# Second MLP of a fused attention + two-MLP kernel: one written order to the end, products gathered into one run per pair, middle block in reverse, six buffers on the way out

## The chip, the cores and the metric

The kernel runs on one core of a Trainium2 chip. The metric is the device time of one execution in microseconds (us). Engines: PE (TensorE, matrix products; its weight loads are listed as PEld), DVE (VectorE), ACT (ScalarE), POOL (GpSimd) and SP, whose queue issues the DMAs here (rows of it are named SPq).

## What is computed

Attention with a sliding window, then two MLPs one after the other, over 2304 tokens of 512 features and 2048 hidden units:

```
attn = softmax(scale*q.k^T + bias, window 128) . v     -> x, 2304 x 512
h = x @ w_in1;    x1 = (s * relu(h)^2 + b) @ w_out1
h = x1 @ w_in2;   out = relu(h)^2 @ w_out2
```

The change concerns the last line alone.

## The kernel before

**Number format.** A value is kept as two float32r halves, high and low, and each product of two values is three matmuls (high.high, high.low, low.high). Weights arrive as 64-bit words and are converted on ACT, DVE and POOL once.

**Tiles.** The second MLP takes the 2304 tokens in three blocks n = 0, 1, 2 of 768 (two halves of 384), and the 2048 hidden units in eight pairs of units of 128, y = 0 to 7. So there are 24 steps k = 8n + y. A step has
- seven first-layer products p1, p2, p6, p5, p7, p4, p3 (a seven-product scheme in place of eight), each of 6 matmuls of 384 columns. p1, p6, p7 and p4 add up in one PSUM bank (`px`), p2, then p5 and p3 in another (`py`). There is one bank of each, so the next step's p1 overwrites what the last one's p4 left in `px`;
- between them the readers of these banks: ACT copies m, u, v out of `px` (tiles `tm`, `tu`, `r_all`) and DVE adds them to `py`; ACT applies relu (j0 to j3, tiles `tr`);
- q0 to q3: DVE squares `tr`, ACT and DVE write its two halves;
- twelve second-layer groups F0 to F11, each of 3 matmuls of 512 columns, which add into six PSUM banks `po` over all eight steps of a block. F0 to F2 need q0, F3 to F5 q1, F6 to F8 q2, F9 to F11 q3. F of step k-1 runs beside the products of step k.

**Waits between products and readers.** p6 adds into the bank that m copies, so it waits for m; p7 waits for u, p4 for v in the same way; p5 overwrites what j0's DVE add reads, p3 adds to what j1's reads; the next step's p1 waits for j2's relu and its p2 for j3's DVE add.

**Weights.** Six pieces per pair, 2.75 MB as float32r halves, are made in block 0 (letters l load, a and b convert, S sums, c split) and stored to DRAM (d). Three sets of places in SBUF hold the pieces of three steps; set k mod 3 serves step k. In blocks 1 and 2 every pair is loaded again (w): 16 pairs.

**Inputs.** Y loads a block's input, Z scales it on ACT, T forms differences on DVE, V splits into halves (ACT copy, DVE subtract of 768 columns); V4 and V3 write the operands of p4 and p3.

**Ways out.** After the eighth step of a block, O0 to O5 copy the six `po` banks to SBUF (ACT and DVE in turn, tiles `ob`) and SP writes them to `out`. O0, O2 and O4 take tag `raw` with 2 buffers, O1, O3 and O5 tag `st` with 3.

**What sets the order.** PE always keeps the order of the program text. The other queues keep it only where a flag (`pinned`) is set; elsewhere a scheduler places their instructions. Block 0 is written out by hand in the table `HANDOVER`, with the flag set: it runs while the first MLP ends, up to some 666 us. Steps 8 to 23 come from the loop at L927, with the flag cleared (L915), and the scheduler may also lift work of the loop into the table's stretch. All instructions are recorded under one line, L29, a helper; so rows are told apart by tiles. In names, `wd` is the DRAM copy of weights, `m2...` the places in SBUF (weights, input halves and the halves of units alike), `acc` the first MLP's result in DRAM.

Of the kernel before, what the change touches and what calls it, by code (L numbers as in the profile page):

```python
# [8 lines left out]
F32 = mybir.dt.float32  # L9
# [6 lines left out]
P = 128  # L16


class InOrder:
# [63 lines left out]
    V1.2 p7.5 W80 V1.6 b7.3 F6.0 d4.5 c7.4 p7.7 d5.3 v7 j7.1 q6.2 w8.0 q7.0 c7.5 w8.5 w9.2 T1.4 w9.1 V1.5 d7.5 V1.7 F6.1 F6.2
    w8.3 F6.3 F6.4 p7.4 p7.3 d7.1 w10.2 w8.4 V1.4 F6.5 V1.3 d6.4 j7.2 F6.6 w10.3 F6.7 F6.8 j7.3 q7.1 F6.9 F6.10 F6.11 w9.4
    q7.2 d6.5 w9.5 d7.4 w10.1 q7.3 w10.0
# [6 lines left out]
def attention_mlp2_kernel(ctx, tc, first0, first1, qkv0, qkv1, qkvt, w_in1, w_out1, s_in, b_in, w_in2, w_out2, out):  # L92
# [604 lines left out]

    BIG, HT, NP = 3 * BLK, 3 * P, NF // 2
# [72 lines left out]
    def load_weights(k, i):  # L771
        sync.dma_start(place_of_weight(k, i).bitcast(F32), wd[k % NP][i])

    def load_input(n, q):
        c, t = divmod(q, 2)
        y = yf[(n, q)] = bp.tile([P, 2, HT], F32, tag="yf", name=f"yf{n}{q}", bufs=5)
        c = slice(2 * c, 2 * c + 2)
        if t == 0:
            sync.dma_start(y[:, :, :BLK], acc_dram[3 * n][:, c, :])
            sync.dma_start(y[:, :, BLK:], acc_dram[3 * n + 1][:, c, :P])  # L780
        else:
            sync.dma_start(y[:, :, :P], acc_dram[3 * n + 1][:, c, P:])
            sync.dma_start(y[:, :, P:], acc_dram[3 * n + 2][:, c, :])
# [211 lines left out]
```

## Time and profile before

| | |
|---|---|
| runs | 934.68 us median of three (934.24 to 935.93) |
| profiled execution | 935.84 us, its span 934.0 us |
| PE busy | 904.3 us, 97% |
| DVE, ACT, POOL busy | 548.4 us, 502.8 us, 102.0 us |
| granted PE clock | 0.99 over the span |

The page lists busy time by engine and forty slices of the span; in all of the second MLP's slices but the last PE shows 9 (90% or more). So the readings that matter are PE's own rows in order of time (start, length of a merged row, and in brackets the idle time before it with what ended it), and beside them the queues that PE waited for. Matmuls overlap in the rows: the distance between two starts is the time that a group costs, not its listed length.

### The profile page before, as it was taken

What the parts mean: (1) busy time and instruction counts of PE and PEld (TensorE: products, weight loads), DVE (VectorE), ACT (ScalarE), POOL (GpSimd) and SP (SyncE); (2) the same over time, 40 slices, a digit from 0 to 9 for tenths busy, and PEclk for the clock granted to TensorE, in tenths of its full rate; (3) what the DMA queues carried; (4) which work ended last, traced back from release to release, by engine and by line L of the source; (5) the groups of instructions that cost most, each with busy time, mean ns of one, the idle gap of its engine ahead of it and who ended that gap; (6) DMA issues with size and microseconds to landing.
All of it is one profiled execution on the core that took longest, in us unless ns stands there. A gap on an engine that the chain in (4) does not pass through costs nothing.

```text
span 934.0 us, 14553 instructions
## 1 busy us (share of the span) xinstructions
PE 904.3 (97%) x5304; PEld 779.1 (83%) x5304; DVE 548.4 (59%) x1321; ACT 502.8 (54%) x1123; POOL 102.0 (11%) x164
## 2 busy tenths in 40 slices
PE   5899999999999999999999999999999999999997
PEld 3789998877787788788898998887889898989896
DVE  6998776455456445544376987787853436443432
ACT  6978775444344444544366876775653335333332
POOL 4343220000000000000022313222000000000000
PEclk8899999999999999999999999999999999999999
DMA  8533523111012101220226665859996656766312
GB/s 315 194 127 133 180 69 114 46 47 40 18 35 91 46 24 46 63 81 16 68 68 217 233 208 184 316 182 349 335 411 203 186 186 183 236 200 192 101 46 68
DMA packets 70216, 136.75 MB, mean 146 GB/s; under 512 B 8576, under 2 KB 36480, under 8 KB 70144
## 3 DMA queue, kind: packets, MB, share of 16 engines
q1 hardware_dynamic: 70144, 135.82, 43.8%
q8 instruction: 42, 0.69, 0.3%
q14 instruction: 30, 0.25, 0.1%
HBM read 103.29 MB, written 32.51 MB: 145 GB/s over the span
## 4 chain that ended last, share of the span: by engine, by line
PE 72%; DVE 11%; ACT 8%; DMA 5%; issue 3%; POOL 0%; SPq 0%; ACTq 0%; DVEq 0%; POOLq 0%
PE ha L29 17%; PE oa L29 17%; PE po L29 16%; PE px L29 8%; PE py L29 6%; PE s L29 6%; DMA st<-w_in 3%; DVE st L29 3%; ACT st L29 2%; DMA st<-w_out 2%; PE u L29 2%; DVE tr L29 1%; PE s_t L29 1%; DVE m2wih L29 1%; DVE r_all L29 1%
## 5 line engine op out<-in xcount | busy, mean ns | idle before, releaser
L29 POOL TENSOR_TENSOR st<-st 128x256 int32<-128x256 int32 x128 | 93.9, 759 | 273.1 <-DVE st L29 247.3
L29 DVE SCALAR_TENSOR_TENSOR r_all<-ha,r_all 128x256 f32<-128x256 f32 (+1 forms) x96 | 52.7, 553 | 103.2 <-ACT r_all L29 103.1
L29 ACT ACTIVATE r_all<-ha 128x256 f32<-128x256 f32 (+1 forms) x96 | 46.3, 485 | 102.4 <-PE ha L29 97.9
L29 ACT ACTIVATE st<-st 128x512 int32<-128x512 uint32 (+3 forms) x100 | 79.7, 813 | 11.0 <-DMA st<-w_in 5.9
L29 PE MATMUL oa<-ga,woh 128*128 128x256 f32 x384 | 72.5, 288 | 0.1
L29 DVE TENSOR_TENSOR tr<-tr 128x384 f32<-128x384 f32 x96 | 55.0, 574 | 22.6 <-ACT tr L29 22.6
L29 ACT ACTIVATE pr<-pr,nd 128x256 f32<-128x256 f32 (+1 forms) x102 | 48.0, 475 | 29.7 <-DVE nd L29 27.6
L29 PEld LDWEIGHTS oa<-ga,woh 128*128 128x128 f32 x384 | 60.1, 191 | 4.6 <-issue 3.5
L29 ACT ACTIVATE tr<-tr 128x384 f32<-128x384 f32 x72 | 37.7, 524 | 40.4 <-DVE tr L29 40.2
L29 PE MATMUL oa<-ga,wol 128*128 128x256 f32 x192 | 54.3, 283 | 0.0
L29 DVE SCALAR_TENSOR_TENSOR st<-st 128x512 int32<-128x512 int32 (+1 forms) x50 | 41.6, 840 | 11.4 <-ACT st L29 10.8
L29 DVE TENSOR_TENSOR tr<-py,tm 128x384 f32<-128x384 f32 x24 | 13.3, 555 | 44.6 <-PE py L29 43.0
L29 DVE TENSOR_TENSOR m2woh<-tr,m2woh 128x384 fp32r<-128x384 f32 x48 | 27.4, 571 | 20.1 <-ACT m2woh L29 18.3
L29 PE MATMUL po<-m2wih,m2woh 128*128 128x512 f32 x144 | 36.6, 395 | 1.3 <-ACT ob L29 0.9
L29 PE MATMUL po<-m2wih,m2wil 128*128 128x512 f32 x144 | 37.8, 392 | 0.0
L29 ACT ACTIVATE m2woh<-tr 128x384 fp32r<-128x384 f32 x48 | 25.2, 525 | 23.2 <-DVE tr L29 22.7
L29 PE MATMUL po<-m2wih,m2wol 128*128 128x512 f32 x144 | 37.6, 392 | 0.0
L29 PE MATMUL ha<-x0h,wih 128*128 128x256 f32 x128 | 37.3, 292 | 0.0
L29 PE MATMUL ha<-x0h,wil 128*128 128x256 f32 x128 | 36.4, 284 | 0.6 <-DVE wil L29 0.6
L29 PEld LDWEIGHTS oa<-ga,wol 128*128 128x128 f32 x192 | 36.7, 191 | 0.0
L29 PE MATMUL ha<-x0l,wih 128*128 128x256 f32 x128 | 36.2, 283 | 0.0
L29 PE MATMUL po<-m2wil,m2woh 128*128 128x512 f32 x144 | 36.0, 393 | 0.0
(606 smaller groups left out, 2404.6 us busy)
## 6 DMA issues: line engine op xcount, KB each, us to landing
m2wih<-wd SPq DMA_DIRECT2D x32, 512.0 KB, 4.6
m2woh<-wd SPq DMA_DIRECT2D x22, 512.0 KB, 4.5
st<-w_out SPq DMA_DIRECT2D x20, 512.0 KB, 4.4
st<-w_in SPq DMA_DIRECT2D x8, 1024.0 KB, 6.4
st<-w_in SPq DMA_DIRECT2D x16, 512.0 KB, 4.4
wd<-m2wih SPq DMA_DIRECT2D x16, 512.0 KB, 6.9
m2wil<-wd SPq DMA_DIRECT2D x16, 512.0 KB, 4.6
st<-w_out SPq DMA_DIRECT2D x6, 1024.0 KB, 7.5
```

Source lines behind the costliest of these rows:

```text
L29: ins = op(*args, **kw)
```

## The change

1. `HANDOVER` loses all stores d5, d6 and d7 and all loads w8, w9 and w10, as well as V1.4, V1.3, q7.1, q7.2 and q7.3; these V and q now stand in the loop's first turn. Nothing else in the table changes its place. Two of its lines, before and after:

```
    d5.1 j6.0 T1.3 T1.2 d6.0 b6.3 F4.6 q5.3 a7.1 d6.1 F4.7 F4.8 F4.9 a7.0 c6.5 b7.1 F4.10 F4.11 p6.5 d5.0 p6.7 F5.0 l7.2 d6.2
    j6.0 T1.3 T1.2 b6.3 F4.6 q5.3 a7.1 F4.7 F4.8 F4.9 a7.0 c6.5 b7.1 F4.10 F4.11 p6.5 p6.7 F5.0 l7.2 b7.0 F5.1 F5.2 v6 p6.4 d4.4
```

2. The flag stays set to the end, so ACT, DVE and SP keep the written order in the loop too.
3. The loop runs to k = 24. One turn is: p4 and p3 of step k-1, then p1, p2, p6, p5, p7 of step k in one run, then all twelve F of step k-1 in one run. q2 is done inside the products, q3, q0 and q1 behind them.
4. In block 1 the pairs go 7, 6, ..., 0. Pairs 7, 6, 5 are still in place from block 0, and pairs 0, 1, 2 are in place when block 2 begins, so five pairs are loaded per block and not eight. Stores d7, d6, d5 are issued in turns 8, 9, 10.
5. O0 to O5 get six buffers (`raw`, `st` and one of `yf`); the last bank's two column halves get a tile each.
6. In block 2 the short tail block of tokens (its rows go out in two DMAs per copy) comes first and not last.

```diff
+    def pair_of(k):
+        n, y = divmod(k, NP)
+        return NP - 1 - y if n == 1 else y
@@ place_of_weight, load_weights
-        tag, n = UNITS[k % 3][2 * i:2 * i + 2]
+        tag, n = UNITS[pair_of(k) % 3][2 * i:2 * i + 2]
-        sync.dma_start(place_of_weight(k, i).bitcast(F32), wd[k % NP][i])
+        sync.dma_start(place_of_weight(k, i).bitcast(F32), wd[pair_of(k)][i])
+    def blocks_of(n):
+        return (LAST, 3 * n, 3 * n + 1) if n == 2 else (3 * n, 3 * n + 1, 3 * n + 2)
@@ way_out
-        ob, i, half = result(f"ob{n}{t}", t % 2 > 0), (6 * n + t) // 2, t % 2
+        i, half = blocks_of(n)[t // 2], t % 2
+            tag = "yf" if x else ("raw", "st", "raw", "st", "yf", "st")[t]
+            ob = bp.tile([P, DM], F32, tag=tag, name=f"ob{n}{t}{x}", bufs={"raw": 2, "st": 3, "yf": 5}[tag])
@@ after the table
     run(table[x] for x in HANDOVER.split())
-    pinned.clear()
@@ the loop
-    for k in range(NP, 3 * NP):
-        do(f"p{k}.1", f"m{k}", f"p{k}.2", f"j{k}.0", f"q{k}.0")
-        behind(k - 1, 0)
-        do(f"p{k}.6", f"u{k}")
-        behind(k - 1, 1)
-        do(f"p{k}.5")
-        behind(k - 1, 2)
-        do(f"p{k}.7", f"v{k}", f"j{k}.1", f"q{k}.1")
-        behind(k - 1, 3, 4, 5)
-        do(f"p{k}.4", f"j{k}.2", f"q{k}.2", f"p{k}.3", f"j{k}.3", f"q{k}.3")
-        behind(k - 1, *range(6, 12))
-        do(*[f"w{k + 3}.{i}" for i in range(4) if k + 3 < 3 * NP], *[f"w{k + 2}.{i}" for i in (4, 5) if k + 2 < 3 * NP])
+    for k in range(NP, 3 * NP + 1):
+        if k > NP:
+            do(f"p{last}.4", f"j{last}.2", f"p{last}.3", f"j{last}.3")
+        if k < 3 * NP:
+            do(f"p{k}.1", f"m{k}", f"p{k}.2", f"j{k}.0", f"p{k}.6", f"u{k}")
+        do(f"q{last}.2")
+            do(f"p{k}.5", f"p{k}.7", f"v{k}", f"j{k}.1", f"r{last}.3", f"r{k}.0")
+                do(f"h{last}.3", f"r{k}.1", f"h{k}.0", f"h{k}.1")
+        if NP <= k < NP + 3:
+            do(*[f"d{2 * NP - 1 - k}.{i}" for i in range(6)])
+        do(*[f"w{a}.{i}" for a in (k + 2,) for i in range(4) if a < 3 * NP and a % NP > 2])
+        behind(k - 1, 0, 1)
+        behind(k - 1, *range(2, 12))
+        do(*[f"w{a}.{i}" for a in (k + 2,) for i in (4, 5) if a < 3 * NP and a % NP > 2])
```

**PE, one turn of the loop (step 13 in block 1).** `px13` and `py13` are products of 6 matmuls, each `po` row one F group of 3. Before:

```order
L29 MATMUL po10_6780<-m2woh0_4840,m2wil2_5554 128x512 x3
L29 MATMUL px13_7218<-m2wol1_5428,m2wol0_4951 128x384 x6
L29 MATMUL po11_6791<-m2woh0_4840,m2wil2_5554 128x512 x3
L29 MATMUL py13_7226<-m2wih3_5444,m2wih1_4987 128x384 x6
L29 MATMUL po12_6801<-m2woh0_4840,m2wil2_5554 128x512 x3
L29 MATMUL px13_7218<-m2wil3_5474,m2wih1_4987 128x384 x6
L29 MATMUL po13_6817<-m2woh0_4840,m2woh2_5587 128x512 x3
L29 MATMUL po14_6821<-m2woh0_4840,m2woh2_5587 128x512 x3
L29 MATMUL po15_6825<-m2woh0_4840,m2woh2_5587 128x512 x3
L29 MATMUL px13_7218<-m2xl1_5441,m2wil0_4791 128x384 x6
L29 MATMUL py13_7226<-m2xh1_5453,m2wol0_4951 128x384 x6
L29 MATMUL po10_6780<-m2woh0_4840,m2woh2_5587 128x512 x3
```

The same place on PE after the change, from step 12's last two products on:

```order
L29 MATMUL px12_7078<-m2xl1_5441,m2wil0_4791 128x384 x6
L29 MATMUL py12_7086<-m2xh1_5453,m2wih0_4778 128x384 x6
L29 MATMUL px13_7190<-m2xh0_5183,m2wil1_5215 128x384 x6
L29 MATMUL py13_7198<-m2xl0_5249,m2wil1_5215 128x384 x6
L29 MATMUL px13_7190<-m2wol1_5428,m2woh1_5218 128x384 x6
L29 MATMUL py13_7198<-m2wih3_5444,m2woh1_5218 128x384 x6
L29 MATMUL px13_7190<-m2wil3_5474,m2woh1_5218 128x384 x6
L29 MATMUL po10_6781<-m2woh0_4840,m2wil2_5554 128x512 x3
L29 MATMUL po11_6785<-m2woh0_4840,m2wil2_5554 128x512 x3
L29 MATMUL po12_6801<-m2woh0_4840,m2wil2_5554 128x512 x3
L29 MATMUL po13_6805<-m2woh0_4840,m2woh2_5587 128x512 x3
L29 MATMUL po14_6809<-m2woh0_4840,m2woh2_5587 128x512 x3
```

Six alternations of products and F groups per step have become one, and five of the seven products now follow a product with no F group between.

**ACT, where the table ends (some 664 us).** `m2xl1` and `m2xh1` are V1.4 and V1.3, `tr2` is j7.2's relu, `tm1` is m8. Before:

```order
L29 ACTIVATE m2wih3_5444<-m2wol3_6295 128x768
L29 ACTIVATE m2wil3_5474<-yf11_5719 128x768
L29 ACTIVATE m2xl1_5441<-yf12_5613 128x768
L29 ACTIVATE m2xh1_5453<-yf13_5949 128x768
L29 ACTIVATE tr2_5573<-px7_6446 128x384
L29 ACTIVATE tm1_5477<-px8_6634 128x384
```

ACT at the same place after the change:

```order
L29 ACTIVATE m2wih3_5444<-m2wol3_6293 128x768
L29 ACTIVATE m2wil3_5474<-yf11_5719 128x768
L29 ACTIVATE tr2_5573<-px7_6434 128x384
L29 ACTIVATE tr3_5583<-tr3_5583 128x384
L29 ACTIVATE tm1_5477<-px8_6587 128x384
L29 ACTIVATE tr0_5489<-tr0_5489 128x384
```

The two splits have moved behind the relu, into the F groups of the loop's first turn; DVE's two subtracts for them have moved with them.

**SP, the loads of the last pair's weights (some 628 us).** `st70` to `st72` are l7.0 to l7.2, `wd` rows are stores. Before:

```order
L29 DMA st70_6304<-w_in2 128x4x256
L29 DMA st71_6313<-w_in2 128x4x256
L29 DMA wd51_4603<-m2woh1_5218 128x1024
L29 DMA wd60_4608<-m2wih0_4778 128x1024
L29 DMA wd61_4609<-m2wih0_4778 128x1024
L29 DMA wd50_4602<-m2wil1_5215 128x1024
L29 DMA st72_6381<-w_out2 128x1024
```

SP after the change:

```order
L29 DMA st70_6302<-w_in2 128x4x256
L29 DMA st71_6311<-w_in2 128x4x256
L29 DMA st72_6375<-w_out2 128x1024
```

Four stores that were issued right behind the two loads are gone from here; they are issued in turns 9 and 10.

## Rows read from the trace of the kernel before

**Rows 1.** The page: the span.

```profile
span 934.0 us, 14553 instructions
```

**Rows 2.** Windows: us, busy (x instructions) per engine, granted clock, DMA share, GB/s.

```profile
634.00:650.00 16.00, 14.35 (x67) 11.31 (x66) 11.46 (x23) 9.82 (x19) 3.18 (x4) 1.00 0.93 350
700.00:750.00 50.00, 50.00 (x252) 45.24 (x251) 18.44 (x34) 16.93 (x35) 0.00 (x0) 1.00 0.65 202
```

**Rows 3.** Timeline of PE, step 13: start, length, instruction, count.

```profile
747.02 1.23 PE L29 MATMUL px<-m2xh,m2wol 128*128 128x384 f32 x6
748.09 1.20 PE L29 MATMUL py<-m2xl,m2wol 128*128 128x384 f32 x6
749.13 0.86 PE L29 MATMUL po<-m2woh,m2wil 128*128 128x512 f32 x3
749.83 1.22 PE L29 MATMUL px<-m2wol,m2wol 128*128 128x384 f32 x6
...
758.59 2.24 PE L29 MATMUL po<-m2woh,m2woh 128*128 128x512 f32 x9
760.67 2.20 PE L29 MATMUL po<-m2woh,m2wil 128*128 128x512 f32 x9
762.72 1.23 PE L29 MATMUL px<-m2xh,m2wil 128*128 128x384 f32 x6
```

**Rows 4.** Timeline, same step: weight load, m's copy, j0's add.

```profile
747.91 1.06 PEld L29 LDWEIGHTS py<-m2xl,m2wol 128*128 128x128 f32 x6
...
748.35 0.49 ACT L29 ACTIVATE tm<-px 128x384 f32<-128x384 f32 x1 [2.96 <-PE px L29]
...
749.40 0.56 DVE L29 TENSOR_TENSOR tr<-py,tm 128x384 f32<-128x384 f32 x1 [3.42 <-PE py L29]
```

**Rows 5.** Timeline of PE: waits between 590 and 700 us.

```profile
594.34 1.33 PE L29 MATMUL px<-m2xh,m2wol 128*128 128x384 f32 x6 [1.04 <-ACT tr L29]
...
666.46 1.31 PE L29 MATMUL px<-m2xh,m2wil 128*128 128x384 f32 x6 [0.69 <-ACT tr L29]
668.36 1.31 PE L29 MATMUL py<-m2xl,m2wil 128*128 128x384 f32 x6 [0.58 <-DVE tr L29]
669.51 0.86 PE L29 MATMUL po<-m2wih,m2wol 128*128 128x512 f32 x3
...
692.92 0.96 PE L29 MATMUL po<-m2wih,m2woh 128*128 128x512 f32 x3 [0.89 <-ACT ob L29]
```

**Rows 6.** Timeline of ACT and DVE ahead of the waits at 666 and 668 us.

```profile
664.45 0.85 ACT L29 ACTIVATE m2xl<-yf 128x768 fp32r<-128x768 f32 x1 [0.22 <-DVE yf L29]
...
665.94 0.47 ACT L29 ACTIVATE tr<-px 128x384 f32<-128x384 f32 x1
...
667.75 0.55 DVE L29 TENSOR_TENSOR tr<-py,tu 128x384 f32<-128x384 f32 x1
```

**Rows 7.** Timeline of SP at l7.0 and l7.1, ACT's wait, and the page's median landing.

```profile
628.04 0.99 SPq L29 DMA_DIRECT2D st<-w_in  x2
...
635.92 1.24 ACT L29 ACTIVATE st<-st 128x512 int32<-128x512 uint32 x2 [2.73 <-DMA st<-w_in]
...
st<-w_in SPq DMA_DIRECT2D x16, 512.0 KB, 4.4
```

**Rows 8.** Timeline of ACT: a lifted pair of Z ahead of the wait at 594 us.

```profile
590.94 1.31 ACT L29 ACTIVATE yf<-yf,bcol,s_sb 128x384 f32<-128x384 f32 x2
```

**Rows 9.** Tile `ob` from 665 to 700 us: its writes to `out`.

```profile
DMA to landing us min/median/max: 6.3/6.7/7.1
```

**Rows 10.** Tile `ob` from 915 us on, and the last two copies in the timeline.

```profile
L29 SPq DMA_DIRECT2D out<-ob x10: 332/546/587, 925.2 to 931.2; - x10
DMA to landing us min/median/max: 2.0/2.1/2.5
928.01 0.42 DVE L29 COPY ob<-po 128x256 f32<-128x256 f32 x1 [0.67 <-PE po L29]
928.47 0.38 ACT L29 ACTIVATE ob<-po 128x256 f32<-128x256 f32 x1 [0.49 <-DVE ob L29]
```

More of the change, by code (lines that the diff above doesn't have):

```diff
@@ L83 @@
[L83 to L85 removed]
+    L0 B L1 G0 H0 G1 l0.0 L2 l0.1 l0.2 H1 L3 a0.0 M a0.1 M0 M1 b0.0 G2 G3 H2 M2 b0.1 S0.0 L4 c0.0 S0.1 a0.2 c0.1 b0.2 c0.3 H3 G4
+    c0.2 H4 L5 l0.3 G5 a0.3 H5 M3 c0.4 b0.3 l1.0 a1.0 b1.0 L6 L7 G6 M4 G7 H6 L8 M5 H7 c0.5 l1.1 l1.2 a1.1 L9 G8 c1.0 b1.1 H8 S1.0
@@ L777, in load_input @@
         c = slice(2 * c, 2 * c + 2)
+        a0, a1, a2 = (acc_dram[i] for i in blocks_of(n))
         if t == 0:
-            sync.dma_start(y[:, :, :BLK], acc_dram[3 * n][:, c, :])
-            sync.dma_start(y[:, :, BLK:], acc_dram[3 * n + 1][:, c, :P])
-        else:
-            sync.dma_start(y[:, :, :P], acc_dram[3 * n + 1][:, c, P:])
-            sync.dma_start(y[:, :, P:], acc_dram[3 * n + 2][:, c, :])
+            sync.dma_start(y[:, :, :BLK], a0[:, c, :])
+            sync.dma_start(y[:, :, BLK:], a1[:, c, :P])
+        else:
+            sync.dma_start(y[:, :, :P], a1[:, c, P:])
+            sync.dma_start(y[:, :, P:], a2[:, c, :])
     def scale_input(n, q, z):
@@ L925, in behind @@
                 do(f"O{k // NP}.{j - 6}")
-    for k in range(NP, 3 * NP):
+    for k in range(NP, 3 * NP + 1):
         n, y = divmod(k, NP)
-        last = n == 2
-        do(f"p{k}.1", f"m{k}", f"p{k}.2", f"j{k}.0", f"q{k}.0")
-        behind(k - 1, 0)
-        do(f"p{k}.6", f"u{k}")
-        behind(k - 1, 1)
-        do(f"p{k}.5")
-        behind(k - 1, 2)
-        do(f"p{k}.7", f"v{k}", f"j{k}.1", f"q{k}.1")
-        behind(k - 1, 3, 4, 5)
-        do(f"p{k}.4", f"j{k}.2", f"q{k}.2", f"p{k}.3", f"j{k}.3", f"q{k}.3")
-        behind(k - 1, *range(6, 12))
-        do(*[f"w{k + 3}.{i}" for i in range(4) if k + 3 < 3 * NP], *[f"w{k + 2}.{i}" for i in (4, 5) if k + 2 < 3 * NP])
-        if not last:
+        last = k - 1
+        if k > NP:
+            do(f"p{last}.4", f"j{last}.2", f"p{last}.3", f"j{last}.3")
+        if k < 3 * NP:
+            do(f"p{k}.1", f"m{k}", f"p{k}.2", f"j{k}.0", f"p{k}.6", f"u{k}")
+        if k == NP:
+            do(f"q{last}.1")
+        do(f"q{last}.2")
+        if k == 3 * NP:
+            do(f"q{last}.3")
+        else:
+            do(f"p{k}.5", f"p{k}.7", f"v{k}", f"j{k}.1", f"r{last}.3", f"r{k}.0")
+            if n < 2 and y == NP - 1:
+                do(f"V{n + 1}.1", f"h{last}.3", f"V{n + 1}.2", f"r{k}.1", f"T{n + 1}.4", f"h{k}.0", f"V{n + 1}.6", f"h{k}.1", f"V{n + 1}.7", f"V{n + 1}.5")
+            else:
+                do(f"h{last}.3", f"r{k}.1", f"h{k}.0", f"h{k}.1")
+        if y == 0 and n < 3:
+            do(*[f"V{n}.{m}" for m in (4, 3)])
+        if NP <= k < NP + 3:
+            do(*[f"d{2 * NP - 1 - k}.{i}" for i in range(6)])
+        do(*[f"w{a}.{i}" for a in (k + 2,) for i in range(4) if a < 3 * NP and a % NP > 2])
+        behind(k - 1, 0, 1)
+        if n < 2:
             if y == 1:
@@ L947, in attention_mlp2_kernel @@
                 do(f"T{n + 1}.1", f"T{n + 1}.2", f"T{n + 1}.3")
-            elif y == 7:
-                do(*[f"V{n + 1}.{m}" for m in (1, 2)], f"T{n + 1}.4", *[f"V{n + 1}.{m}" for m in (6, 5, 7, 4, 3)])
-    behind(3 * NP - 1, *range(12))
+        behind(k - 1, *range(2, 12))
+        do(*[f"w{a}.{i}" for a in (k + 2,) for i in (4, 5) if a < 3 * NP and a % NP > 2])
 def kernel(q, k, v, moe_w_in, moe_w_out, moe_s, moe_b, moe2_w_in, moe2_w_out):
```

51 lines of the change are left out of this document (26 added, 25 removed).

## The prediction

> **What bounds the kernel now.** I read the span first [rows 1], then windows by stage, then PE's own rows, since PE is the engine that is always busy. From 700 us on PE has no idle time at all (50.00 of 50.00 us) while DVE and ACT work for little more than a third of it and DMA for two thirds [rows 2]. So three things can shorten the kernel: groups of matmuls that cost less, waits of PE before some 700 us, and what comes after PE's last matmul.
>
> The groups: in step 13 two products in a row cost 748.09 - 747.02 = 1.07 and 749.13 - 748.09 = 1.04 us, one F group among products 749.83 - 749.13 = 0.70, and nine matmuls (three F groups) 2.09 where the stretch begins and 762.72 - 760.67 = 2.05 where it goes on, 0.683 per group [rows 3]. The whole step lasts 762.72 - 747.02 = 15.70 us. A product behind a product thus costs 1.04 and not some 1.065, an F group behind an F group 0.683 and not 0.70: an alternation costs about 0.04 us.
>
> The waits: four stand out between 590 and 700 us (1.04, 0.69, 0.58, 0.89) [rows 5], and the window from 634 to 650 us lacks 16.00 - 14.35 = 1.65 us of PE at a DMA share of 0.93 [rows 2].
>
> The end: PE stops just ahead of the DVE copy at 928.01 that waited for it, the last ACT copy begins at 928.47 and waited for the DVE copy of the same bank, the last of ten writes is issued at 931.2, and the span ends at 934.0 [rows 1, 10].
>
> **The change, part by part.** Nothing is computed that was not computed before; the counts of matmuls, copies and splits stay, 36 loads of weights and one write fall away.
>
> *Gathered products, steps 8 to 23.* Before, a step has six alternations, after it has one. New step: a product behind F 1.065, six behind products 6 x 1.04 = 6.24, the first F group 0.70 and eleven of 0.683 = 7.51: together 15.51 us against 15.70, 0.19 saved, times 16 steps = **3.0 us** [rows 3].
>
> The same edit takes F groups away from between products, and with them the cover of the readers. Each of five waits per step is now covered by one product, 1.04 us. The price of the answers: ACT's copy of `px` begins 748.35 - 748.09 = 0.26 after the product gives way, takes 0.49, and PE goes on 0.05 later (copy 665.94 + 0.47 = 666.41, PE at 666.46): 0.80 us. DVE's add begins 0.27 after its product (749.40 - 749.13), takes 0.56, and PE follows 0.06 later (667.75 + 0.55 = 668.30, PE at 668.36): 0.89 us [rows 4 to 6]. Both are below 1.04. But the weights of a group's first matmul are loaded 0.18 us ahead of it (747.91 against 748.09) [rows 4], so the answer is wanted after 0.86 us: ACT makes that with 0.06 to spare, DVE misses it by 0.03, twice per step. What a missed load costs at most is seen where PE really waited: the product at 668.36 took 669.51 - 668.36 = 1.15, 0.11 above 1.04 [rows 5]. So two misses cost between 0 and 2 x 0.03 x 16 = 1.0 us; I take **0.3 lost**, nearer to nothing, since a miss of 0.03 is a small part of the 0.18. Squares and halves wait behind this on DVE and ACT, but their F groups come 2 to 6 us later, and both engines are idle for more than half of a step [rows 2].
>
> The Trainium skill (Perfetto Trace Analysis, section Optimizing Tensor Performance) speaks against this edit: independent groups should rotate through PSUM banks, so that the reading of one overlaps the next one's matmuls; here seven groups in a row use two banks. The answers of 0.80 and 0.89 us above, within one product's 1.04, say that two banks just suffice.
>
> *V1.4, V1.3 and q7 out of the table.* At 666.46 p8.1 waited 0.69 for the relu of `px` (ACT, 665.94), which stood behind two splits of 0.85 us that begin at 664.45; at 668.36 p8.2 waited 0.58 for DVE's add (667.75), behind the same splits' subtracts [rows 5, 6]. With the splits moved behind, ACT reaches the relu some 1.5 us earlier, and DVE its add likewise; both waits go, and with them about 0.1 of restart each: **1.5 us**. The splits now lie in the F groups of the loop's first turn, 8 us long, and p8.4 wants them only after that. They are late by nothing there.
>
> *Six buffers.* At 692.92 an F group of block 1 waited 0.89 us for an ACT copy of block 0's bank; its buffer was the third use of two, and writes to `out` took 6.3 to 7.1 us to land there [rows 5, 9]. Six buffers end that, and F of step 8 also comes a product run later: 0.89 plus a restart of 0.1, **1.0 us**.
>
> *Stores and loads out of the table.* ACT waited 2.73 us for l7.0 or l7.1, issued at 628.04 and used at 635.92, 7.9 us after the issue, where the median of these loads is 4.4 [rows 7]. Four stores, 2 MB, were issued right behind them and are gone. If the loads land at the median, ACT begins about 3 us earlier, and the waits of 634 to 650 us, which follow from ACT and DVE being late after this, could go whole: 1.65 us and restarts, at most 2.0 [rows 2]. If the loads were slow for traffic issued earlier, nothing goes. DVE is busy for 11.46 of these 16 us, so some waits may come back at another place. I take **1.2 us** (0 to 2.0).
>
> *Lifted Z.* Ahead of the wait at 594.34 stood a pair of Z of block 2, 1.31 us of ACT [rows 5, 8], which the scheduler had lifted; in written order it comes in turn 11. But a load that ACT needs stands between this pair and the copy, so I take **0.3 us** (0 to 0.9).
>
> *SP.* The stores of pairs 7, 6, 5 (8.25 MB), the five pairs of loads and Y2 now meet in turns 8 to 12. Up to the load of the second pair that is some 16 MB, 46 us at the 350 GB/s of the stretch where DMA was 0.93 busy [rows 2]; counted from turn 8's start at some 665 they are done by about 718 with what SP waits between, and that pair is wanted at turn 12, near 727. Cost 0, cover some 9 us.
>
> *The end.* In block 2 the bank rows that need two writes per copy now come first. Behind the last matmul there were four short writes and the second of a pair; now there are two. Ten issues went from 925.2 to 931.2 and took 0.33 to 0.59 each [rows 10]. New: the last matmul at E, DVE's half copied by E + 0.46; SP is then some 0.4 behind from the four 0.59 issues at the front, so the last write is issued at about E + 1.3, where it was 931.2 - 928.0 = E + 3.2. The last two are twice as large, 2.5 and not 2.0 us to landing [rows 10]. So 1.9 - 0.3 = **1.6 us** (1.2 to 1.9). The separate tile for the last half brings nothing: ACT still waits for DVE on that bank, and SP is the later of the two.
>
> **Sum:** 3.0 - 0.3 + 1.5 + 1.0 + 1.2 + 0.3 + 1.6 = 8.3 us. The profiled execution's 935.84 would be 927.5; it was 1.16 above the median, so against the median 934.68 - 8.3 = **926.4 us**. With every term at its better end (no miss, 2.0, 0.9, 1.9) 10.3 us, 924.4; at its worse end (1.0 lost, 0, 0, 1.2) 5.7 us, 929.0.
>
> **Rivals.**
> 1. *The alternation costs nothing.* The differences of 0.02 us between neighbours may belong to the places of the operands or to the stamps, and the step stays at 15.70. For it: only a few hundredths each. Against it: they recur in every step and p2 and p3 alike, the two products that follow a product, are the cheap ones [rows 3]. Then 8.3 - 2.7 = 5.6 us, **929.1**. The Trainium skill (TensorE: Matmul & The Clock Gate, section Back-to-back issue gap) gives an isolated matmul N/2.4 + 2.5 ns, whatever stands beside it; by that a step would cost the same in both orders, an estimate of 42 x 162.5 + 36 x 215.8 = 14.6 us. The rows show 15.70, so something besides columns costs time.
> 2. *The product run stalls (slower).* Place: p1, p2, p6, p5 and p7 in each of 16 steps, 80 waits, each covered by one product. For it: a margin of -0.03 to 0.06 us, and in-order ACT queues m behind j3's relu with nothing to spare. Against it: DVE and ACT are empty at that place. A wait that is late by 0.1 us each time, restart included, costs 80 x 0.1 = 8 us and eats the whole gain; from 0.104 on the kernel is slower. At 0.13 it is 10.4 us, **936.8**. If only the two DVE answers fail whole, 32 x 0.11 = 3.5, 929.6.
> 3. *SP in written order is late.* One wait for the buffers of six stores behind the ways out, and the loads of the pairs at turns 11 and 12 miss by as much. If my 9 us of cover are gone and 4 us miss, **930.4**.
>
> **How the numbers follow.** Forecast 926.4 with its bounds 924.4 to 929.0: 0.66. Rival 1: 0.13. Rival 2: 0.10, half of it with the waits late by less than 0.1 us each (928 to 934), half slower than before. Rival 3: 0.04. Still more gained than the best ends: 0.07. The range 923.8 to 930.5 takes in the forecast's bounds, rival 1, the milder rival 2 and rival 3's example. About 0.2% (1.9 us) is what a measurement of this kernel tells from no change: faster 0.91, same 0.04, slower 0.05.
>
> **What would show it.** In the profile after: steps of 15.5 us between two p1, with products 1.04 apart and F groups 0.68; PE idle of a few tenths in all from 665 us to its end; no wait for `ob`; ACT's wait for `st<-w_in` near 633 us of less than 1 us; the last write issued 1.3 us behind PE's end and the span's end 4.4 us behind it, where it was 6.0. I am wrong if PE waits for `tr`, `tm` or `tu` recur in each step, if the step stays at 15.7, or if PE waits for a DMA of `m2...<-wd`.

## The result, and the profile after

The changed kernel takes 925.82 us (median of four runs, 924.48 to 926.89) against 934.59 before (four runs, 934.24 to 935.93): ratio 0.9903, interval 0.9886 to 0.992, 8.8 us faster. The forecast was 926.4, its range 923.8 to 930.5.

The four runs of the changed kernel differ by some 1.2 us either way. Between traces most of such a difference is there by 100 us: the first product of step 0 (p1, the anchor below) begins at 534.38 us in the trace after, at 536.77 in that before, and between 534.8 and 537.8 in the experiments, though no instruction ahead of it was changed, and PE's matmul that begins at 99.64 us in the trace after begins at 101.59 in that before and between 99.9 and 102.9 in the others. Why is open; the granted clock differs in that stretch too (0.93 to 0.98 from 20 to 100 us), but the traces with the higher clock are not always the early ones. So terms of 1 us are read here from stretches between starts of p1 and not from whole times. From that anchor to the span's end it is 397.2 us before and 388.3 after, 8.9 us less.

| stretch, us | before | after |
|---|---|---|
| steps 0 to 4 (p1 of step 0 to p1 of step 5) | 70.23 | 70.64 |
| steps 5 to 7 | 59.46 | 55.73 |
| step 8 | 16.64 | 15.62 |
| step 9 | 16.84 | 15.51 |
| steps 10 to 22, thirteen | 204.02 | 201.62 |
| p1 of step 23 to PE's last matmul | 24.01 | 23.87 |
| PE's last matmul to the span's end | 6.03 | 5.33 |

The page after, its span (before: [rows 1]):

```profile
span 922.7 us, 14395 instructions
```

PE's timeline after, step 13 (start, length, instruction, count; before: [rows 3]):

```profile
738.40 1.20 PE L29 MATMUL px<-m2xh,m2wil 128*128 128x384 f32 x6
739.44 1.20 PE L29 MATMUL py<-m2xl,m2wil 128*128 128x384 f32 x6
740.48 1.20 PE L29 MATMUL px<-m2wol,m2woh 128*128 128x384 f32 x6
...
743.60 2.24 PE L29 MATMUL po<-m2woh,m2wil 128*128 128x512 f32 x9
745.68 4.24 PE L29 MATMUL po<-m2woh,m2woh 128*128 128x512 f32 x18
749.76 2.20 PE L29 MATMUL po<-m2woh,m2wil 128*128 128x512 f32 x9
751.80 1.23 PE L29 MATMUL px<-m2xl,m2xh 128*128 128x384 f32 x6
...
753.91 1.20 PE L29 MATMUL px<-m2xh,m2wol 128*128 128x384 f32 x6
```

The step is 753.91 - 738.40 = 15.51 us, to the hundredth what was forecast; a product behind a product costs 1.04 (739.44 to 740.48), with or without a reader between. The tightest answer is DVE's add (j0), for which p5 waits:

```profile
740.73 0.56 DVE L29 TENSOR_TENSOR tr<-py,tm 128x384 f32<-128x384 f32 x1 [1.58 <-PE py L29]
741.35 1.05 PEld L29 LDWEIGHTS py<-m2wih,m2woh 128*128 128x128 f32 x6
```

It ends at 741.29, 0.81 behind its product (740.48), and the weights of p5 are loaded at 741.35, at their usual time. All waits of PE over 0.15 us from 480 us to the end (us in total, times, longest):

```profile
PE px L29 <- ACT tr L29: 1.4, 1, 1.4
PE ha L29 <- DVE r_all L29: 0.5, 1, 0.5
PE px L29 <- ACT tm L29: 0.4, 1, 0.4
PE px L29 <- DVE m2wol L29: 0.3, 1, 0.3
```

None lies in the loop. The windows that answer to [rows 2]:

```profile
634.00:650.00 16.00, 15.71 (x76) 13.31 (x76) 12.95 (x24) 9.81 (x19) 4.71 (x6) 1.00 0.60 198
```

PE lacks 0.29 us there and not 1.65, at a DMA share of 0.60 and not 0.93. ACT's wait for l7.0 and l7.1 is this now (2.73 in [rows 7]):

```profile
631.03 1.25 ACT L29 ACTIVATE st<-st 128x512 int32<-128x512 uint32 x2 [0.29 <-DMA st<-w_in]
```

Two things came out otherwise. At step 4 the wait of 1.04 [rows 5] grew. ACT, then PE:

```profile
590.75 1.22 ACT L29 ACTIVATE st<-st 128x512 int32<-128x512 uint32 x2 [2.23 <-DMA st<-w_in]
591.85 0.49 ACT L29 ACTIVATE tr<-px 128x384 f32<-128x384 f32 x1
592.40 1.31 PE L29 MATMUL px<-m2xh,m2wol 128*128 128x384 f32 x6 [1.44 <-ACT tr L29]
```

The lifted pair of Z is gone from there, and ACT idles in its place for a load. And at the end [rows 10] the writes still queue up. PE, SP, DVE, ACT, and the landing of the writes to `out` from 905 us on:

```profile
915.17 2.20 PE L29 MATMUL po<-m2wih,m2wol 128*128 128x512 f32 x9
...
914.63 5.36 SPq L29 DMA_DIRECT2D out<-ob  x9
...
917.41 0.42 DVE L29 COPY ob<-po 128x256 f32<-128x256 f32 x1 [0.67 <-DMA out<-ob]
917.86 0.38 ACT L29 ACTIVATE ob<-po 128x256 f32<-128x256 f32 x1 [0.54 <-DVE ob L29]
...
L29 SPq DMA_DIRECT2D out<-ob x9: 394/546/667, 914.6 to 919.3; - x9
DMA to landing us min/median/max: 2.3/2.4/2.7
```

PE ends at 915.17 + 2.20 = 917.37 (E); nine issues follow one another from 914.63 to 919.99, the last begins at E + 1.95.

### The profile page after: what moved, and what is told of

It reads as the page before. It is cut to its first block, busy times and chain, and to the rows that moved or that the text cites. A ratio compares the mean times of both kernels' runs of the same rounds, so it can differ in the third digit from the quotient of the medians.

```text
span 922.7 us, 14395 instructions
## 1 busy us (share of the span) xinstructions
PE 896.5 (97%) x5304; PEld 776.2 (84%) x5304; DVE 545.4 (59%) x1321; ACT 499.5 (54%) x1123; POOL 102.3 (11%) x164
## 4 chain that ended last, share of the span: by engine, by line
PE 74%; DVE 10%; ACT 8%; DMA 4%; issue 2%; POOL 0%; SPq 0%; ACTq 0%; DVEq 0%; POOLq 0%
PE ha L29 17%; PE oa L29 17%; PE po L29 17%; PE px L29 8%; PE py L29 6%; PE s L29 5%; DVE st L29 3%; ACT st L29 2%; DMA st<-w_in 2%; DMA st<-w_out 2%; PE u L29 2%; PE s_t L29 1%; DVE tr L29 1%; DVE m2wih L29 1%; DVE r_all L29 1%
## 5 line engine op out<-in xcount | busy, mean ns | idle before, releaser
L29 DVE TENSOR_TENSOR tr<-py,tu 128x384 f32<-128x384 f32 x24 | 13.3, 556 | 77.8 <-PE py L29 77.6
L29 DVE TENSOR_TENSOR tr<-tr 128x384 f32<-128x384 f32 x96 | 52.9, 565 | 0.0
L29 ACT ACTIVATE tr<-px 128x384 f32<-128x384 f32 x24 | 11.7, 487 | 71.8 <-PE px L29 71.4
L29 PE MATMUL po<-m2woh,m2woh 128*128 128x512 f32 x162 | 38.8, 390 | 0.0
L29 PE MATMUL po<-m2wil,m2woh 128*128 128x512 f32 x162 | 38.8, 390 | 0.0
L29 PEld LDWEIGHTS po<-m2wil,m2woh 128*128 128x128 f32 x162 | 30.4, 188 | 6.2
```

What stands on the lines that cost most here:

```text
L29: ins = op(*args, **kw)
```

## The experiments

Each is the changed kernel with the edit shown, but for the last, which is the kernel before with one edit. Times of the kernel before beside them lay at 933.8 to 937.8, median 934.4 to 934.9.

### The loop's order

**Five runs of F per step.** The F groups go back among the products:

```diff
-        if k > NP:
-            do(f"p{last}.4", f"j{last}.2", f"p{last}.3", f"j{last}.3")
...
-            do(f"p{k}.1", f"m{k}", f"p{k}.2", f"j{k}.0", f"p{k}.6", f"u{k}")
+            do(f"p{k}.1", f"m{k}", f"p{k}.2", f"j{k}.0")
+            behind(last, 0)
+            do(f"p{k}.6", f"u{k}")
+            behind(last, 1)
...
+            do(f"p{k}.5")
+            behind(last, 2)
...
-        behind(k - 1, *range(2, 12))
+        behind(k - 1, 5)
+        if k < 3 * NP:
+            do(f"p{k}.4", f"j{k}.2", f"p{k}.3", f"j{k}.3")
+        behind(k - 1, *range(6, 12))
```

> The changed kernel with one thing undone: in each turn of the loop the F groups stand again among the products (F0 behind p2, F1 behind p6, F2 behind p5, F3 to F5 behind p7, F6 to F11 behind p4 and p3), so five runs of F per step and not one. Everything else stays as in the changed kernel. Theory (an alternation of products and F groups costs time): the step from p1 to p1 goes from 15.51 back to 15.68 to 15.70 us, no engine waits, and the kernel is 15 x 0.18 = 2.7 us slower than the changed one, some 928.5. Rival (alternation costs nothing, the shorter step came from fewer waits or from something else in the new order): steps stay at 15.51, and the time at 925.8.

Measured: 940.62 us, ratio 1.0074 (1.0055 to 1.0094). The steps 10 to 15 take 94.16 us as before, 15.69 each: alternation costs what was read from [rows 3]. But the kernel is 12 us slower than forecast here, at two places: step 8 takes 19.27 and step 16 22.21. PE at step 8:

```profile
674.25 0.45 PE L29 MATMUL px<-m2xl,m2wil 128*128 128x384 f32 x1 [2.46 <-ACT m2xl L29]
```

With p4 in the same turn as V4, nothing covers the split. (Step 16 has a wait of 1.12 us for j3's DVE add as well.) So a second kernel makes V4 and V3 of the next block a turn earlier:

```diff
-        if y == 0 and n < 3:
+        if k == NP:
             do(*[f"V{n}.{m}" for m in (4, 3)])
@@ behind p4 and p3
+        if n < 2 and y == NP - 1:
+            do(*[f"V{n + 1}.{m}" for m in (4, 3)])
```

> The kernel e1_five_runs (changed kernel with five runs of F groups per step) with one mend: V4 and V3 of the next block, which stood in the same turn ahead of the p4 that reads them, now stand a turn earlier, behind the last step's p4 and p3, so that they have F6 to F11 and the next products as cover. Theory (alternation costs 0.18 us per step, and the rest of that kernel's loss, 3.6 us at step 8 and 6.7 us at step 16, were waits of PE for V4 and V3 alone): steps 15.69 throughout, step 16 back at 15.7, no wait of PE for m2xl there; step 8 keeps its wait, since its V4 and V3 are still made in the loop's first turn; some 3 us for the steps and 3.6 for step 8 slower than the changed kernel, 932.5. Rival (step 16 lost its time to the ways out or to loads that share the queue): step 16 stays near 22 us, 939.

Measured: 936.23 us, ratio 1.0012 (1.0001 to 1.0022). No wait for `m2xl` at step 16, which falls from 22.21 to 17.73 us, not to 15.7: the wait for j3's DVE add, which stands behind the block's other splits, is still there (1.10), and one of 0.39 for m, behind the splits that were moved, is new. Step 8 takes 20.88 and not 19.27, though its waits are the same 2.46 and 0.55: behind them the granted clock is 0.80 (674.6 to 678 us) and 0.74 (678 to 682), where with five runs alone it was 1.00. The steps between are 15.69 again. So the gathered order is worth 2.9 us by itself, and its cut, p4 and p3 a whole F run behind p7, gives the splits of a new block a cover that five runs don't have.

**Gathered in the kernel before, nothing else.** All seven products of step k in one run, then the F of step k - 1:

```diff
-        behind(k - 1, 0)
         do(f"p{k}.6", f"u{k}")
-        behind(k - 1, 1)
         do(f"p{k}.5")
-        behind(k - 1, 2)
         do(f"p{k}.7", f"v{k}", f"j{k}.1", f"q{k}.1")
-        behind(k - 1, 3, 4, 5)
         do(f"p{k}.4", f"j{k}.2", f"q{k}.2", f"p{k}.3", f"j{k}.3", f"q{k}.3")
-        behind(k - 1, *range(6, 12))
+        behind(k - 1, *range(12))
```

> The kernel before with one part of the change alone: in the loop all seven products of a step stand in one run and all twelve F groups of the step ahead behind them; table, flag, buffers, pairs, stores and loads as before. Theory (the gathered order is worth its 3.0 us by itself, and it also hides the ways out, since seven products stand between a block's last F group and the next one's first): steps of 15.51 us, the wait of 0.89 for an ob copy gone, the waits at the table's end (0.69 and 0.58) still there: 3.0 + 0.9 = 3.9 us faster than the kernel before, 930.8. Rival (the gathered order needs the written order on the other queues): PE waits in the steps or at the block boundaries eat the gain, 934 or more.

Measured: 950.76 us, ratio 1.0165 (1.0146 to 1.0184), slower than before: steps of 16.43, and 17.97 and 18.09 for steps 8 and 15. ACT's v, then PE's p7, p4 and p3 in step 13:

```profile
754.70 0.49 ACT L29 ACTIVATE r_all<-px 128x384 f32<-128x384 f32 x1 [0.85 <-PE px L29]
...
753.39 1.21 PE L29 MATMUL px<-m2wil,m2wih 128*128 128x384 f32 x6
755.24 1.32 PE L29 MATMUL px<-m2xl,m2wil 128*128 128x384 f32 x6 [0.64 <-ACT r_all L29]
756.40 1.20 PE L29 MATMUL py<-m2xh,m2wol 128*128 128x384 f32 x6
```

p4 comes right behind p7 and waits for v with no product between: 755.24 - 753.39 - 1.04 = 0.81 us for ACT's whole answer, and the product behind the wait takes 756.40 - 755.24 = 1.16, 0.12 more than 1.04. 15.51 + 0.81 + 0.12 = 16.44 is the step. The missing piece is not the written order: in the steps, the products that have one product as cover don't wait here, and with the flag cleared in the changed kernel (below) most steps stay near 15.5. It is where the run is cut. The changed kernel cuts it between p7 and p4, so that v has twelve F groups as cover.

**Later answers.** ACT's copies m, u, v are preceded by a second copy of the first N columns, N = 64 and N = 384:

```diff
+        if k > NP:
+            act_copy(temp(nm)[:, :N], pairs[(k, "x")][:, :N])
         act_copy(temp(nm), pairs[(k, "x")][:, :HT])
```

> The changed kernel with ACT's three copies m, u and v of steps 9 to 23 each preceded by a second copy of the first 64 columns of the same bank to the same place, so that the answer to PE comes some 0.2 us later: about 1.0 us behind the product, which is still within the next product's 1.04 us, but later than that product's successor wants its first weights (0.86). Theory (a missed load of weights costs up to 0.11 us): 45 misses, the step grows from 15.51 by 0.1 to 0.33 us, up to 5 us in all, 931. Rival (only the 1.04 us of the covering product count): the step stays at 15.51 to 15.55, below 0.6 us in all, 926.

> The changed kernel with ACT's three copies m, u and v of steps 9 to 23 each done twice, all 384 columns, so that the answer to PE comes 0.45 us later, at about 1.25 us behind the product, past the next product's end at 1.04. Both theories want waits here, three per step. Lateness with a restart on top (0.21 + 0.11): the step grows by 0.96 to 16.5 us, 15 steps, some 14 us, 940. Lateness alone: 0.63 per step, 9.5 us, 935. Rival (the queues hide it, for instance since the copies begin earlier than thought): the step stays at 15.51, 926.

Measured: 929.37 (two runs, ratio 0.9938, 0.9918 to 0.9957) and 936.68 us (ratio 1.0017, 1.0006 to 1.0027). Steps of 15.64 and 16.17, 0.13 and 0.66 more. PE and ACT with N = 64:

```profile
743.42 1.21 PE L29 MATMUL py<-m2xl,m2wil 128*128 128x384 f32 x6
744.41 0.99 PEld L29 LDWEIGHTS px<-m2wol,m2woh 128*128 128x128 f32 x6
744.46 1.27 PE L29 MATMUL px<-m2wol,m2woh 128*128 128x384 f32 x6
745.56 1.21 PE L29 MATMUL py<-m2wih,m2woh 128*128 128x384 f32 x6
...
743.61 0.75 ACT L29 ACTIVATE tm<-px 128x64 f32<-128x64 f32 x2
```

and PE with N = 384:

```profile
744.61 1.21 PE L29 MATMUL py<-m2xl,m2wil 128*128 128x384 f32 x6
745.87 1.31 PE L29 MATMUL px<-m2wol,m2woh 128*128 128x384 f32 x6
747.02 1.20 PE L29 MATMUL py<-m2wih,m2woh 128*128 128x384 f32 x6
```

With N = 64 the copy ends 743.61 + 0.75 - 743.42 = 0.94 us behind its product. p6 begins on time, 1.04 behind p2, but its weights are loaded only 744.46 - 744.41 = 0.05 us ahead of it (0.17 to 0.18 elsewhere), and it takes 1.10: a late load of weights costs 0.06, and no row shows a wait. With N = 384 p6 begins 1.26 behind p2, 0.22 late, and takes 1.15: 0.22 + 0.11 = 0.33, lateness with a restart. Both come twice per step, for m and u (2 x 0.06 and 2 x 0.33); the expectations counted v as well, which has the F groups as cover. So a late load of weights does cost something, and only the margin of the changed kernel's answers keeps it at nothing.

**The flag cleared behind the table.**

```diff
     run(table[x] for x in HANDOVER.split())
+    pinned.clear()
```

> The changed kernel with the flag cleared after the table, as before, so that the scheduler places the loop's instructions of ACT, DVE and SP (PE keeps the written order). Theory of the prediction (the written order on these queues as such brings little: PE order, the emptier table and the buffers do it; the lifted Z cost nothing by the changed kernel's trace): steps stay at 15.51, the wait ahead of p1 of step 4 stays between 0.9 and 1.4 us, the time is within 1 us of the changed kernel's 925.8. Rival (the written order is what keeps readers ahead of squares, splits and halves): PE waits of 0.2 to 0.7 us return in the steps or at the block boundaries, 2 to 10 us slower.

Measured: 936.6 us, ratio 1.0017 (1.0004 to 1.0029), 10.8 us above the changed kernel. The theory was wrong. The trace is that of the slowest of ten runs (940.92 us): from the anchor on it loses 14.9 us to the changed kernel's trace. The steps away from the blocks' ends stay near 15.5; 6.0 us are lost in steps 8 and 9, 7.8 in steps 5 to 7. ACT, then PE, in step 9:

```profile
691.96 1.30 ACT L29 ACTIVATE yf<-yf,bcol,s_sb 128x384 f32<-128x384 f32 x2 [1.94 <-DMA yf<-acc]
693.17 0.47 ACT L29 ACTIVATE tu<-px 128x384 f32<-128x384 f32 x1
...
693.69 2.29 PE L29 MATMUL px<-m2wil,m2wil 128*128 128x384 f32 x6 [2.81 <-ACT tu L29]
695.78 2.83 PE L29 MATMUL po<-m2wih,m2wil 128*128 128x512 f32 x9
```

The scheduler put Z of block 2 ahead of u, and Z waits for a load. The other is the table's stretch: from 596 to 618 us the DMA share is 0.77 (0.51 in the changed kernel), stores of the loop were lifted into it, a load lands late, and PE waits 2.04 us for v; steps 5 to 7 take 63.57.

### The table, the buffers, the end

**Splits back.** `p7.4 p7.3 F6.5 j7.2` in the table becomes `p7.4 p7.3 V1.4 F6.5 V1.3 j7.2`, and turn 8 leaves V4 and V3 out.

> The changed kernel with V1.4 and V1.3 (ACT copies and DVE subtracts of 128 x 768) back in the table ahead of j7.2 and j7.3, as before. Theory (the splits made ACT's relu and DVE's add late): PE waits again where step 8 begins, 0.6 to 0.9 us for the relu ahead of p8.1 and up to 0.6 for the add ahead of p8.2, so that the lead over the kernel before falls by 0.9 to 1.5 us between step 7 and step 9, and the time is 1 to 1.5 us longer than that of the changed kernel. Rival (the waits came from the DMA traffic of that stretch, the splits ran anyway in idle time): no wait of PE over 0.2 us there, same time.

Measured: 927.79 us (ratio 0.9926, 0.9911 to 0.994). Both waits of [rows 5] are back:

```profile
662.83 1.31 PE L29 MATMUL px<-m2xh,m2wol 128*128 128x384 f32 x6 [0.73 <-ACT tr L29]
664.73 1.32 PE L29 MATMUL py<-m2xl,m2wol 128*128 128x384 f32 x6 [0.58 <-DVE tr L29]
```

The 0.73 lies ahead of step 8's p1, and step 8 takes 16.51 and not 15.62: 0.73 + 0.89 = 1.6 us. The theory held; the loss is a little above its 1 to 1.5 us (2.0 by the medians).

**Two buffers.** The third use of `raw` for O4 of blocks 0 and 1:

```diff
-            tag = "yf" if x else ("raw", "st", "raw", "st", "yf", "st")[t]
+            tag = "yf" if x else ("raw", "st", "raw", "st", "raw" if n < 2 else "yf", "st")[t]
```

> The changed kernel with O4 of blocks 0 and 1 in tag raw again, which has two buffers, so that its copy waits until O0's write to out has landed. Theory of the prediction (the buffers end the wait of 0.89 us that PE had at 692.92): ACT's copy for O4 waits for a DMA, and PE waits again for an ob copy at the first F groups of step 8 and of step 16, 0.5 to 1 us each, so 1 to 2 us slower than the changed kernel. Rival 1 (the product run hides it: between the last F of a block and the first F of the next one there are now seven products, 7.3 us): ACT waits for the DMA as before, PE does not, 0. Rival 2 (the wait came from the traffic that made writes land late, 6.3 to 7.1 us before and 2.0 to 2.8 after): landing stays near 2.3 us, ACT waits less than 1 us, PE not at all, 0.

Measured: 926.58 us (ratio 0.9914, 0.9899 to 0.9929). Steps 8 and 9 take 15.58 and 15.51, no wait for `ob`: the prediction's theory fell. The writes land after 2.0 to 2.8 us here, and no copy waits for one, so rival 2's condition holds. But rival 1 suffices without it: the gathered kernel before has two buffers too, its writes land late, and PE doesn't wait for `ob` either. Tile `ob` there, 670 to 700 us, and the F groups of block 1's first step:

```profile
DMA to landing us min/median/max: 5.5/5.7/8.4
...
691.70 2.24 PE L29 MATMUL po<-m2wih,m2wil 128*128 128x512 f32 x9
```

So the seven products between the blocks' F groups, rival 1, are enough to end the wait of 0.89 us. Nor was the buffer what the copy of O4 waited for last in the kernel before. ACT there:

```profile
690.74 0.49 ACT L29 ACTIVATE r_all<-px 128x384 f32<-128x384 f32 x1 [2.38 <-PE px L29]
...
692.28 0.58 ACT L29 ACTIVATE ob<-po 128x512 f32<-128x512 f32 x1
```

O0's write, whose buffer O4 takes, was one of the first two, issued by 682.2; at the longest landing of [rows 9], 7.1 us, it was done by 689.3. ACT was idle then, until 690.74, and had v and a relu to do before the copy: the copy was late by its place in the order that the scheduler chose.

**Stores back**, four of them, or all eighteen of pairs 5 to 7 at their old places:

```diff
-    ... l7.0 p6.2 l7.1 m6 p6.6 ...
+    ... l7.0 p6.2 l7.1 d5.1 d6.0 d6.1 d5.0 m6 p6.6 ...
```

> The changed kernel with four of the stores (two pieces of pair 5, two of pair 6, 2 MB in all) back in the table right behind the loads of pair 7's first two weight pieces, and gone from the loop's turns. Theory (these stores make the two loads land late, and ACT with them): the loads, issued near 625, are used some 7.5 to 8 us later in place of 5.5, ACT waits about 2.5 us for them and not 0.3, and the window from 634 to 650 us loses 1 to 2 us of PE; the lead over the kernel before falls by as much there, and the time is 1 to 2 us longer. Rival (the loads were late for traffic issued earlier or later than these four, the loads of w9 and w10 among it): ACT's wait stays below 1 us and the window keeps 15.5 us of PE or more.

> The changed kernel with all 18 stores of pairs 5, 6 and 7 back in the table at their old places, and gone from the loop's turns; the loads of w8, w9 and w10 stay out. Four of these stores alone, right behind the loads l7.0 and l7.1, brought ACT's wait for these loads only to 1.25 us, while kernels without them showed 0.25 to 1.40. Theory (the whole of the stores' traffic, two of them issued near 610 and 617, ahead of these loads, delays loads for ACT): ACT's wait at l7.0 and l7.1 is 2 us or more, the stretch from p1 of step 5 to p1 of step 8 takes 58 us or more, as in the kernel before (58.8 without the wait for the splits), 2 to 3 us above the changed kernel's 55.7. Rival (the loads w8 to w10 were the traffic that mattered): the stretch stays at 55.7 to 57.0 us, as without the stores.

Measured: 927.9 (ratio 0.9923, 0.9908 to 0.9938) and 927.95 us (0.9921, 0.9905 to 0.9938). ACT at l7.0 and l7.1 with four stores, then with all:

```profile
634.15 1.25 ACT L29 ACTIVATE st<-st 128x512 int32<-128x512 uint32 x2 [1.25 <-DMA st<-w_in]
...
634.80 1.27 ACT L29 ACTIVATE st<-st 128x512 int32<-128x512 uint32 x2 [1.51 <-DMA st<-w_in]
```

Steps 5 to 7 take 57.04 and 57.61 us. The kernels without these stores (the wait for the splits taken off) lie at 55.65 to 56.03 in six traces and at 56.96 and 56.98 in two (the last try below, which moves a conversion in this stretch, aside), and these two (five runs, two buffers) show waits of 1.21 and 1.40 at l7.0 and l7.1 without any store. So the four stores alone, which the prediction named, can't be told from what varies without them. All eighteen cost 0.6 to 2.0 us, and a wait of PE near 617 us, 0.41 in the kernel before, comes back with them (0.45; 0.20 with four stores, under 0.15 in the kernels without). The kernel before stands at 59.46 - 0.69 = 58.77. The rest, 1.2 us, can't be put down to the loads w8 to w10. In the gathered kernel before, PE, ACT and SP do the same instructions in the same order as in the kernel before from p1 of step 0 to p1 of step 8, these loads among them, and the stretch takes 58.34 - 0.70 (its wait for the splits) = 57.64 us. ACT at l7.0 and l7.1 there:

```profile
634.88 1.25 ACT L29 ACTIVATE st<-st 128x512 int32<-128x512 uint32 x2 [1.26 <-DMA st<-w_in]
```

So the wait of 2.73 us of [rows 7] is 1.26 in another execution of the same instructions, and this stretch varies by 1.1 us with them.

**Tail block last again.**

```diff
-        return (LAST, 3 * n, 3 * n + 1) if n == 2 else (3 * n, 3 * n + 1, 3 * n + 2)
+        return 3 * n, 3 * n + 1, 3 * n + 2
```

> The changed kernel with the blocks of tokens in the old order in block 2, so that the short tail block, whose rows go out in two writes per copy, comes last again. Theory of the prediction (the last writes queue on SP): last write issued 3.2 us behind PE's end and not 1.95, the span's end 6.0 us behind it as in the kernel before and not 5.3; some 0.7 us longer than the changed kernel. The prediction's own figure would be 1.6 longer, since it put the end at E + 4.4. Rival (the end is set by the landing of the last write and the engines' closing, whatever the order of the blocks): still 5.3 us from PE's end to the span's end, 0.

Measured: 927.38 us (ratio 0.9918, 0.9903 to 0.9933). PE's end to the span's end is 6.24 us, 0.9 more than in the changed kernel, and the last of ten issues begins 3.14 us behind PE's end:

```profile
L29 SPq DMA_DIRECT2D out<-ob x10: 332/546/592, 916.6 to 922.5; - x10
```

**A try at more.**

```diff
-    ... l5.1 a5.1 b5.0 j3.2 ...
+    ... l5.1 j3.2 a5.1 b5.0 ...
-    ... a6.3 l7.0 p6.2 l7.1 m6 p6.6 ...
+    ... l7.0 p6.2 l7.1 m6 a6.3 p6.6 ...
+                by = scalar if n == 2 and (t, x, a) in ((0, 0, 1), (2, 0, 0), (5, 1, 0)) else sync
```

> A try at a faster version: the changed kernel with three moves. (a) In the table j3.2, ACT's relu for which p1 of step 4 waits, stands ahead of a5.1, the conversion that waits for a load of weights. (b) m6, ACT's copy for which p6 of step 6 waits 0.4 us, stands ahead of a6.3, which waits for another load. (c) Three of the last block's writes (the second of O0, O2's, and the last half's) are issued on ACT's queue and not on SP's. Theory (ACT's in-order queue stood behind loads, and SP's issues queue up behind the end): the waits of 1.0 to 1.4 us at step 4 and of 0.4 at step 6 go; the last write is issued 1 us earlier and the span ends 4.2 to 4.6 us behind PE and not 5.3; 2 to 2.7 us faster than the changed kernel, 923 to 924. Rival for (a) (the load is wanted by what follows anyway, so the wait comes back at p2 or at step 5): the stretch from step 0 to step 5 stays at 70.4 us. Rival for (c) (landing and closing set the end): still 5.3 us.

Measured: 927.92 us (ratio 0.9926, 0.9914 to 0.9939): no gain. Steps 0 to 4 take 70.77 us, the wait has moved from p1 to p2, and the writes on ACT's queue hold up ACT's copies. DVE ahead of p2, PE, then ACT's queue and ACT at the end:

```profile
593.46 0.69 DVE L29 SCALAR_TENSOR_TENSOR st<-st 128x512 int32<-128x512 int32 x1 [2.12 <-ACT st L29]
...
595.01 1.31 PE L29 MATMUL py<-m2xl,m2wol 128*128 128x384 f32 x6 [0.95 <-DVE tr L29]
...
917.68 2.25 ACTq L29 DMA_DIRECT2D out<-ob  x1
...
920.02 0.60 ACT L29 ACTIVATE ob<-po 128x512 f32<-128x512 f32 x1 [2.38 <-PE po L29]
```

j3's add on DVE stands behind a conversion that waits, by way of ACT, for the same load. Only the wait for m6 went. PE's end to the span's end is 5.69 us, longer than 5.33.

## Why the prediction was right, and where not

The sum was 8.3 us, the trace shows 8.9 from the anchor on and the medians 8.8. Term by term:

- **Gathered products**, 3.0: right. 204.02 - 201.62 = 2.40 for thirteen steps, 0.14 at the end, about 0.19 in each of steps 8 and 9: 2.9. Undone twice, the steps went back to 15.69. (The prediction counts six alternations; the order has five runs of F. The 0.19 came from the lengths, so the sum stands.) Here the same 78 matmuls take 15.69 or 15.51 us by their order, so rival 1 fell. The Trainium skill (TensorE: Matmul & The Clock Gate, section Back-to-back issue gap) gives a gap for an isolated matmul that depends on the columns alone; that figure doesn't carry over to these rows.
- **Product run**, -0.3: nothing was lost. The rows after show the product behind each answer at 1.04. DVE's add begins 0.25 behind its product and not 0.27, so that the predicted miss of 0.03 is none. The mechanism is real all the same: an answer 0.2 us later costs 0.06 per wait, one 0.45 later 0.33. By the Trainium skill (Perfetto Trace Analysis, section Optimizing Tensor Performance) independent groups should rotate through banks; two banks sufficed here at answers of 0.8 us, and at 1.26 they cost 0.66 per step. No run shows what more banks would do.
- **Splits out of the table**, 1.5: right, 1.6 by undoing it.
- **Six buffers**, 1.0: right in size (step 9: 16.84 - 15.51 = 1.33, less 0.19 for the order, 1.1), wrong in owner. Two buffers do as well; the later F, which the prediction named second, is enough to earn it, and in the kernel before ACT's order held the copy up after the buffer was free. A term of the buffers is 0.
- **Stores and loads out of the table**, 1.2 (0 to 2.0): too small for the two traces compared, 58.77 - 55.73 = 3.0 us. The gathered kernel before, with the same table, gives 57.64 - 55.73 = 1.9, and other pairs of traces with and without the stores 0.6 to 3.1. So the size is known to a microsecond at best, and whether the upper bound of 2.0 was too low is open. Two things in its working don't hold: it took the idle time of one window, 634 to 650, while PE also lost some 0.4 near 617, where two of the stores go out earlier (610 and 617); and it took the 2.73 us of one trace as what the stores and loads cost.
- **Lifted Z**, 0.3 (0 to 0.9): nothing. Steps 0 to 4 take 69.99 to 70.77 us in all kernels, with Z there or not. The doubt in the text, the load that stands between, was the whole answer.
- **SP**, 0: right, PE never waits for `m2...<-wd`.
- **The end**, 1.6 (1.2 to 1.9): 6.03 - 5.33 = 0.7. The failed step is "SP is then some 0.4 behind": the first half was copied by E + 0.46 (917.41 + 0.42 = 917.83) and its write was issued at 918.82, 1.0 behind, so that the last one began at E + 1.95 and not E + 1.3. The four short issues at the front cost what was read for them, 0.55 to 0.60; the issues behind them, whole tiles and a half, took 0.39 to 0.53, where whole tiles that stood 0.6 to 0.8 apart had taken 0.33 [rows 10], and the last half took 0.67. The 0.3 taken off for the larger last writes is 0.5 by the prediction's own figures, 2.5 and 2.0. The order of the blocks as such is worth 0.9, by undoing it.

So the terms that can be undone one by one, the gathered products and the splits, were right with their mechanism, and the total came out by errors that cancel in these two traces, which is luck: 1.8 us too little for the stores, 0.9 too much for the end and 0.7 for steps 0 to 4 (-0.4 and not 0.3). The largest thing the prediction didn't see is the flag: priced at 0.3 for Z, it is worth 10.8 us in the new kernel by the medians. It was judged by what the scheduler had lifted in the kernel before; with the table emptied and the F gathered, the scheduler has other things to lift, and lifts them.

## To carry over

A gain read from neighbouring rows (an alternation of 0.04 us) held here because it recurs in every step, but the order that earns it must be cut where the slowest answer has its cover: the same gathering with p4 behind p7 made the kernel before 16 us slower. Price a written order by what a scheduler could lift in the new program, not by what it lifted in the old one. And where an engine's queue stands behind a load, moving one instruction ahead moves the wait to the next reader of the same load.

## What was not expected of the hardware

- Long waits of PE can bring a second loss. Behind the wait of 2.81 us above, with the flag cleared, the product at 693.69 took 695.78 - 693.69 = 2.09 us and not 1.04; the granted clock in that stretch is the lower of the two levels, 1.2 GHz:

```profile
693.60:696.60 3.00, 2.91 (x8) 2.76 (x9) 1.49 (x2) 2.28 (x6) 0.00 (x0) 0.51 0.84 307
```

  The product behind the wait of 2.04 us in that kernel took 2.09 too. Behind the wait of 1.44 us at 592.40 in the changed kernel it took 593.55 - 592.40 = 1.15. The length of the wait alone doesn't decide it: the waits of 2.46 and 0.55 at step 8 left the clock at 1.00 with five runs alone and were followed by 0.80 and 0.74 in the second kernel, where this is the 1.6 us between 19.27 and 20.88. The same two figures stand behind the waits of 2.52 and 0.54 at step 16 with five runs alone. So rival 2's price per wait is not one figure.
- The first of three writes that ACT issued took 2.25 us, the others 0.34 and 0.36; SP's at that time took 0.33 to 0.60. No run shows why.
